# ReLU² attention, Fourier mix and feed-forward on one core: batch 0's rows with a PSUM tile for each half, the first feed-forward groups in two token passes, and the scores of batch 2 held back

## The chip, the cores and the metric

The kernel runs on one core of a Trainium2 chip. The metric is the device time in microseconds (us) of one execution. A core has five engines that run side by side, each through its own list of instructions in a fixed order: PE (matmul), ACT (functions of one operand, with scale and bias), DVE (elementwise work and statistics), POOL (elementwise work and indirect DMA) and SP (which issues DMA). An instruction waits until what it reads is there and what it overwrites is free; all that stands behind it on its engine waits with it. PE writes to PSUM, which is small: here it holds three tiles of two banks, called psS, and two tiles of one bank, called psF.

## The reference

```python
batch, n_heads, seq, head_dim = (8, 12, 448, 64)          # d_model 768, w_ch1 768x3072, w_ch2 3072x768

def _attn_ref(q, k, v):
    scores = scale * np.matmul(q, k.transpose(0, 1, 3, 2))  # scale = 1/sqrt(64)
    attn = np.maximum(scores, 0.0) ** 2 / S
    return np.matmul(attn, v)

def _moe_ref(x, w_ch1, w_ch2):                             # x: the heads side by side, (8, 448, 768)
    mixed = np.real(np.fft.fft(np.fft.fft(x, axis=1), axis=2))
    u = x + mixed
    un = (u - mean(u)) / np.sqrt(var(u) + 1e-06)           # over the last axis
    ch = np.maximum(un @ w_ch1, 0.0) @ w_ch2
    return u + ch
```

## The kernel before

For each batch the kernel computes scores (L537), ReLU on ACT (L558), the square on DVE (L564) and the product with v (L522) for six pairs of heads. `fold` (L445 to L456) turns the result into x with channels on partitions, xT, and into sums and differences of mirrored tokens. The Fourier transform of real data is symmetric, so both transforms are matmuls with half-size cosine and sine tables: over the channels (L961, result copied to `pc`, L977), then over the tokens (L805 in `mix_rows`). A tile of rows stands for a range of tokens from the first half of the sequence ("top", HS = 224 tokens) and its mirror image ("bottom"). For batches 1 to 7 `mix_rows` makes tm, tp, u = x + mixed, its statistics (L837), the scale and the shift (rstd, nmr L846), and the normalized `un` (ACT for batch 1, POOL for later ones, L854). u and un are stored to DRAM (utop and ntop by SP; ubot and nbot by an indirect DMA of POOL that puts the mirrored rows in order, L879).

The feed-forward part, `ffn`, takes tokens in groups: group 0 is the first 384 tokens of batch 0, group 1 the last 64 of batch 0 and all 448 of batch 1, and so on in pairs of 384 and 512. Its input is unT, with channels on partitions. For batches 2 to 7 it comes by a transposing DMA (L902, from ntop and nbot) issued by SP; SP also issues the transposes of x (xn<-xT, L477) and of q and k (qkT<-qkr, L398), the reloads of u into `o` (L1034) and the stores of the output (L1061). For batches 0 and 1 PE transposes un by a matmul with an identity `ident` or a mirrored identity `rev` (L708, L775), and DVE or ACT copy the result to unT (L723, L780). FFN1 (L1073) has 24 blocks of 6 matmuls; each block fills one psF bank with 384 or 512 columns, and a ReLU (L1044 on DVE, L1046 on ACT) writes hT. FFN2 (L1091) accumulates 24 matmuls of 384 columns into a psF bank; DVE adds u (L1054).

Batch 0 has a tail of its own, `first_tail`, because nothing else can run on PE until its first rows are ready. There are four tiles of rows, t = 0 to 3: top tokens 0 to 127 and their mirror, then 112 more of each. `rows` makes both halves (of 384 channels) of a tile into one psS tile (t = 0 to 2) or the two psF banks (t = 3): per half 4 matmuls of 384 columns (L605) and 3 of 128 (L609) that add x. `stats` (L629), `aggregate` (L635), `root` (ACT, L641), `scale` (L649, L650), `copy` (u to SBUF, L658), `norm` (POOL L682, ACT L684, DVE L687), `turn` (transposes, L708) and `unload` (copy to unT, L723) follow, in an order written out by hand. `turn` also issues matmuls on a constant tile `warm` whose result is used by nobody:

```python
for i in range(k):                     # k = 5 in turn 1, 3 in turn 2: 256 columns each (L706)
    nc.tensor.matmul(bank[0][:, 0:256], lhsT=warm[:, 0:128], rhs=warm[:, 0:256], ...)
for i in range(16 if t == 1 else 0):   # 128 columns each (L713)
    nc.tensor.matmul(bank[0][:, 384:512], lhsT=warm[:, 0:128], rhs=warm[:, 0:128], ...)
```

The order on each engine elsewhere is decided when the program is built, by a planner, `Streams`. Each part of the kernel is a generator that asks by `need(engine, duration, dependencies, buffers, condition)` for its next step; the planner takes the step that can start earliest by its own reckoning, a step whose condition is false only if nothing else is left, and on a tie the smaller rank. The durations are estimates in the code, for a matmul of n columns `mm(n)` = n/2400 + 0.006. `progress` counts the feed-forward work planned so far, and attention of a batch may run ahead of it by LEAD. Attention of batch 1 is held while the tail is being written out (`tail[0]` is 1).

Of the kernel before, what the change touches and what calls it, by code (L numbers as in the profile page):

```python
# [117 lines left out]
def mm(n):  # L118
    return n / 2400 + 0.006
# [18 lines left out]
def kernel(  # L138
# [54 lines left out]
    back = [const.tile([128, 1], mybir.dt.int32, name=f"back{i}") for i in range(2)]  # L193
    warm = const.tile([128, 512], BF16, name="warm")
# [27 lines left out]
    def mirrors():  # L222
        nc.gpsimd.memset(rev, 0.0)
        nc.gpsimd.affine_select(out=rev, in_=rev, compare_op=ALU.not_equal, fill=1.0,
                                base=-127, pattern=[[1, 128]], channel_multiplier=1)
        nc.gpsimd.iota(back[0], pattern=[[0, 1]], base=HS, channel_multiplier=-1)

        v = const.tile([128, 2], FP32, name="backv")
# [253 lines left out]
    def attention(b):  # L482
# [5 lines left out]
        while pa < NB:  # L488
# [23 lines left out]
            e = yield need("PE", dur + SWITCH, deps, bufs, lambda: progress[0] >= lead and (b != 1 or tail[0] == 2 or tail[0] == 0 and p < 0))  # L512
# [68 lines left out]
    def first_tail(pcs):  # L581


        pus, helds, done, sts = [None] * 4, [None] * 4, [[None, None] for _ in range(4)], [None] * 4
        mvs, stds, rss, nms, uts, pts = ([None] * 4 for _ in range(6))
        t_st, t_mv, t_std, t_rn = ([0.0] * 4 for _ in range(4))
        t_un, t_u = [[0.0, 0.0] for _ in range(4)], [[0.0, 0.0] for _ in range(4)]

        def rows(t):
            ch, i = divmod(t, 2)  # L590
            s0, s1 = SC[ch]
            n = s1 - s0
            d = 4 * mm(D // 2) + 3 * 0.06
            e = yield need("PE", 2 * d, [pcs[0][1], pcs[1][1]] + x_ready[0], [BF, BF] if t == 3 else [BS])
            if t == 3:
                pu = helds[t] = [BF.take() for _ in range(2)]
            else:
                helds[t] = [BS.take()]
                pu = [helds[t][0][:, 0], helds[t][0][:, 1]]
            for hf in range(2):  # L600

                for w in range(2):
                    for a, (n0, n1) in enumerate(TC):
                        mat = seq[:n1 - n0, w, a, s0:s1] if w == 0 or i ^ hf else nseq[:n1 - n0, a, s0:s1]
                        nc.tensor.matmul(pu[hf][:n, 0:D // 2], lhsT=mat,  # L605
                                         rhs=pcs[a][0][:n1 - n0, w, hf:hf + D // 2],
                                         start=(w == 0 and a == 0), stop=False)
                for a in range(3):
                    nc.tensor.matmul(pu[hf][:n, a * 128:(a + 1) * 128],  # L609
                                     lhsT=xTc[5 - a if hf else a][:, i * XH + s0:i * XH + s1],  # L610
                                     rhs=rev if hf else ident, start=False, stop=(a == 2))
                done[t][hf] = e - (1 - hf) * d + LATENCY["PE"]
            pus[t] = [p[:n] for p in pu]
            if t == 3:
# [5 lines left out]
        def half(t, hf):  # L620

            return pus[t][hf][:, D // 2 - 1::-1] if hf else pus[t][hf][:, 0:D // 2]

        def stats(t, hf):
            n = SC[t // 2][1] - SC[t // 2][0]
            t_st[t] = yield need("DVE", dve(D // 2), [done[t][hf]])
            if hf == 0:
                sts[t] = work.tile([128, 2, 6], FP32, name="stats", tag="stats", bufs=2)
            nc.vector.bn_stats(sts[t][:n, hf, :], pus[t][hf][:, 0:D // 2])  # L629

        def aggregate(t):
            n = SC[t // 2][1] - SC[t // 2][0]
            t_mv[t] = yield need("DVE", 0.2)
            mvs[t] = work.tile([128, 2, 2], FP32, name="mv", tag="mv", bufs=4)[:n]
            nc.vector.bn_aggr(mvs[t][:, 0, :], sts[t][:n])  # L635

        def root(t):
            n = SC[t // 2][1] - SC[t // 2][0]
            t_std[t] = yield need("ACT", 0.25, [t_mv[t] + LATENCY["DVE"]])
            stds[t] = work.tile([128, 2], FP32, name="std", tag="std", bufs=4)[:n]  # L640
            nc.scalar.activation(stds[t][:, 0:1], mvs[t][:, 0, 1:2], AF.Sqrt, bias=eps_t[:n])  # L641

        def scale(t):
            n = SC[t // 2][1] - SC[t // 2][0]
            e = yield need("DVE", 0.3, [t_std[t] + LATENCY["ACT"]])
            t_rn[t] = e + LATENCY["DVE"]
            rss[t] = work.tile([128, 2], FP32, name="rstd", tag="rstd", bufs=4)[:n, 0:1]
            nms[t] = work.tile([128, 2], FP32, name="nmr", tag="nmr", bufs=4)[:n, 0:1]
# [3 lines left out]
        def copy(t, hf, en):  # L652
            ch, i = divmod(t, 2)
            n = SC[ch][1] - SC[ch][0]
            e = yield need(en, (act if en == "ACT" else dve)(D // 2), [done[t][hf]], [BU[i]] if hf == 0 else [])
            if hf == 0:
                uts[t] = work.tile([128, D], FP32, name="u", tag=f"u{i}" if i else "u", bufs=2)
            (nc.scalar.copy if en == "ACT" else nc.vector.tensor_copy)(  # L658
                uts[t][:n, hf * (D // 2):(hf + 1) * (D // 2)], half(t, hf))
            t_u[t][hf] = e  # L660
            if t == 3:
                BF.give(helds[t][hf], e)
            if hf == 1:
                if t != 3:
                    BS.give(helds[t][0], max(t_u[t]))
                e = max(t_u[t])
                first_us[ch][i] = uts[t], e + LATENCY["ACT"], e
                u_done[ch][i].t = e + LATENCY["ACT"]

        def norm(t, hf, en):  # L670
            ch, i = divmod(t, 2)
            n = SC[ch][1] - SC[ch][0]
            deps = [t_rn[t]]
            if en == "POOL":
                deps.append(u_done[ch][i])
            d = {"ACT": act(D // 2), "DVE": dve(D // 2), "POOL": 2.0}[en]
            e = yield need(en, d, deps, [BUN[ch]] if i == 0 and hf == 0 else [])
            if uns[0][t] is None:
                uns[0][t] = work.tile([128, D], BF16, name="un", tag=f"un{t}", bufs=1)
            un = uns[0][t][:n]  # L680
            if en == "POOL":
                nc.gpsimd.tensor_scalar(un, uts[t][:n], rss[t], nms[t], op0=ALU.mult, op1=ALU.add)  # L682
            elif en == "ACT":
                nc.scalar.activation(un[:, hf * (D // 2):(hf + 1) * (D // 2)], half(t, hf), AF.Identity,  # L684
                                     bias=nms[t], scale=rss[t])
            else:
                nc.vector.tensor_scalar(un[:, hf * (D // 2):(hf + 1) * (D // 2)], half(t, hf), rss[t], nms[t],  # L687
                                        op0=ALU.mult, op1=ALU.add)
            t_un[t][hf] = e + LATENCY[en]
            if min(t_un[t]) or en == "POOL":  # L690
                half_un[ch][i].t = max(t_un[t])

        def turned_cols(t):

            return ((128, ident, 0, 128), (128, rev[:, 0:63], HS + 97, 63),
                    (96, ident[:96, :96], 128, 96), (97, rev[:97, 31:128], HS, 97))[t]

        def turn(t, k):
            n, idn, c0, w = turned_cols(t)
            un = uns[0][t]  # L700
            e = yield need("PE", 6 * 0.06 + 0.11 * k, [max(t_un[t])], [BS])
            pts[t] = [BS.take()]
            bank = [pts[t][0][:, 0], pts[t][0][:, 1]]
            for i in range(k):

                nc.tensor.matmul(bank[0][:, 0:256], lhsT=warm[:, 0:128], rhs=warm[:, 0:256], start=True, stop=True)  # L706
            for m in range(MC):
                nc.tensor.matmul(bank[m // 3][:, m % 3 * 128:m % 3 * 128 + w], lhsT=un[:n, m * 128:(m + 1) * 128],  # L708
                                 rhs=idn, start=True, stop=True)
            done[t] = [e + LATENCY["PE"]] * 2  # L710
            for i in range(16 if t == 1 else 0):

                nc.tensor.matmul(bank[0][:, 384:512], lhsT=warm[:, 0:128], rhs=warm[:, 0:128], start=True, stop=True)  # L713
            if t == 1:
                yield need("PE", 16 * 0.055)

        def unload(t, en):
            n, idn, c0, w = turned_cols(t)
            g = groups[0][2]
            src = pts[t][0][:, :, 0:384].rearrange("p h (m w) -> p h m w", w=128)[:, :, :, 0:w]  # L720
            dst = g[:, :, c0:c0 + w].rearrange("p (h m) w -> p h m w", h=2)
            last = yield need(en, (act if en == "ACT" else dve)(6 * w), [done[t][0]])
# [440 lines left out]
```

## Time and profile before

| | before |
|---|---|
| time, median of 3 runs | 610.66 us (610.34 to 611.09) |
| span of the profiled execution | 607.4 us |
| instructions in the profile | 10224 |
| granted PE clock, in every stretch read | 1.000 |
| rows of batch 0 begin on PE | 41.06 us |
| FFN1 of group 0 begins | 53.74 us |
| FFN1 of group 1 begins | 126.67 us |
| FFN1 of group 2 begins | 210.68 us |

The span is that of one profiled execution, from its first to its last instruction; the page gives no other time for it. The median of the runs is 3.26 us longer than the span. All starts below are counted from the start of the span. An engine's share of busy time is an average over the whole span; what a wait costs is read in its place on the timeline.

### The profile page before, as it was taken

How to read it: one execution, taken by the hardware profiler on the slowest of the kernel's cores; microseconds unless marked ns; L12 is line 12 of the kernel's file. 1: busy time of each engine (PE TensorE's matmuls, PEld its weight loads, DVE VectorE, ACT ScalarE, POOL GpSimd, SP SyncE). 2: the span in 40 equal slices, each digit the busy share in tenths (PEclk: the TensorE clock that was granted, in tenths of full speed). 3: DMA queues.
4: the chain of work that ended last, by engine and by line, in shares of the span. 5: the costliest groups of instructions: out<-in, count | busy, mean ns of one | idle time of the engine just before them, and what ended most of it. 6: DMA issues, size and time to landing. Idle time of an engine off the chain costs nothing.

```text
span 607.4 us, 10224 instructions
## 1 busy us (share of the span) xinstructions
PE 595.4 (98%) x4035; PEld 329.5 (54%) x4054; DVE 339.4 (56%) x766; ACT 293.3 (48%) x445; POOL 155.2 (26%) x200
## 2 busy tenths in 40 slices
PE   8999999989999999999999999999999999999997
PEld 7566556534555565555445565555445566654464
DVE  6977785876596568455834369645843447110011
ACT  5967661677544357436653167435761345014300
POOL 8433203311163137111710117210620006100000
PEclk9999999999999999999999999999999999999999
DMA  9999997888659967977593796985451215420022
GB/s 127 207 209 228 216 194 132 186 128 120 111 148 212 157 121 215 141 135 120 172 154 96 127 127 173 160 164 97 145 136 60 87 51 165 121 91 20 1 79 79
DMA packets 125216, 82.22 MB, mean 135 GB/s; under 512 B 76272, under 2 KB 113168, under 8 KB 125168
## 3 DMA queue, kind: packets, MB, share of 16 engines
q0 software_dynamic: 40320, 34.07, 34.4%
q1 hardware_dynamic: 84848, 47.50, 33.6%
q8 instruction: 32, 0.52, 0.4%
q14 instruction: 16, 0.13, 0.1%
HBM read 62.91 MB, written 26.69 MB: 148 GB/s over the span
## 4 chain that ended last, share of the span: by engine, by line
PE 83%; DVE 11%; ACT 4%; issue 1%; DVEq 0%; ACTq 0%
PE psF L1091 33%; PE psF L1073 32%; PE psF L522 6%; PE psS L537 6%; DVE sq L564 2%; PE psS L961 2%; ACT sq L558 2%; DVE stats L837 2%; PE psS L1113 1%; PE psS L805 1%; DVE u L826 1%; DVE u L825 1%; PE psS L605 1%; PE psF L421 1%; DVE tm L816 1%
## 5 line engine op out<-in xcount | busy, mean ns | idle before, releaser
L1073 PE MATMUL psF<-unT,w 128*128 128x384 bf16 (+1 forms) x1134 | 227.2, 352 | 1.4 <-issue 0.2
L558 ACT ACTIVATE sq<-psS 112x896 bf16<-112x896 f32 x192 | 164.8, 916 | 130.5 <-PE psS L537 130.4
L1091 PE MATMUL psF<-w,hT 128*128 128x384 bf16 (+2 forms) x1343 | 225.0, 326 | 0.8 <-DVE xT L448 0.7
L1091 PEld LDWEIGHTS <-hT 128*128 128x128 bf16 x1344 | 129.2, 98 | 93.4 <-issue 8.8
L1073 PEld LDWEIGHTS <-w 128*128 128x128 bf16 x1152 | 109.6, 98 | 109.3 <-issue 12.3
L1046 ACT ACTIVATE hT<-psF 128x512 bf16<-128x512 f32 (+1 forms) x180 | 98.6, 548 | 110.2 <-PE psF L1073 109.6
L564 DVE TENSOR_TENSOR sq<-sq 112x896 bf16<-112x896 bf16 x192 | 117.8, 635 | 44.6 <-ACT sq L558 43.3
L1054 DVE TENSOR_TENSOR o<-psF,o 128x384 f32<-128x384 f32 (+2 forms) x56 | 31.0, 553 | 106.2 <-PE psF L1091 105.9
L300 POOL DMA_DIRECT2D vn<-in_v_dram x24 | 17.3, 719 | 177.4 <-PE psF L522 156.9
L445 DVE TENSOR_SCALAR xT<-psF 128x224 bf16<-128x224 f32 x48 | 18.7, 389 | 71.7 <-PE psF L522 71.7
L537 PE MATMUL psS<-qkT 64*112 64x448 bf16 x384 | 52.3, 366 | 2.0 <-DVE unT L780 0.8
L522 PE MATMUL psF<-sq,vn 112*64 112x448 bf16 x384 | 45.9, 359 | 1.7 <-DVE sq L564 1.2
L825 POOL TENSOR_TENSOR u<-tp,xn 128x385 f32<-128x385 f32 (+1 forms) x14 | 15.5, 1108 | 117.0 <-DVE tp L816 94.7
L537 PEld LDWEIGHTS <-qkT 64*112 64x112 bf16 x384 | 20.8, 125 | 27.6 <-issue 21.6
L522 PEld LDWEIGHTS <-vn 112*64 112x64 bf16 x384 | 17.9, 109 | 24.2 <-issue 16.0
L854 POOL TENSOR_SCALAR un<-u,rstd,nmr 128x768 bf16<-128x768 f32 (+1 forms) x24 | 26.9, 1124 | 6.4 <-DVE nmr L846 6.0
L837 DVE BATCH_NORM_STATS2 stats<-u 128x6 f32<-128x384 f32 (+1 forms) x56 | 28.2, 539 | 0.0
L879 POOL DMA_INDIRECT ubot<-u,back x16 | 17.1, 1072 | 23.7 <-DVE hT L1044 19.3
L300 POOL DMA_DIRECT2D qn<-in_q_dram x21 | 15.3, 726 | 19.7 <-DVE qkr L389 10.8
L1113 PE MATMUL psS<-warm 128*128 128x126 bf16 (+1 forms) x204 | 17.9, 242 | 1.3 <-DVE warm L215 1.3
L448 DVE TENSOR_SCALAR xT<-psF 128x224 bf16<-128x224 f32 x48 | 18.4, 384 | 0.0
L456 DVE TENSOR_TENSOR fold<-xT 128x225 bf16<-128x225 bf16 x48 | 15.9, 331 | 2.1
(117 smaller groups left out, 369.1 us busy)
## 6 DMA issues: line engine op xcount, KB each, us to landing
out_dram<-o SPq DMA_DIRECT2D x27, 384.0 KB, 2.7
vn<-in_v_dram POOLq DMA_DIRECT2D x24, 224.0 KB, 5.0
qn<-in_q_dram POOLq DMA_DIRECT2D x21, 224.0 KB, 6.3
kn<-in_k_dram POOLq DMA_DIRECT2D x21, 224.0 KB, 7.2
w<-in_moe_w_ch_dram POOLq DMA_DIRECT2D x12, 384.0 KB, 14.1
w<-in_moe_w_ch_dram POOLq DMA_DIRECT2D x4, 1152.0 KB, 22.7
utop<-u SPq DMA_DIRECT2D x8, 384.0 KB, 2.6
o<-utop SPq DMA_DIRECT2D x8, 384.0 KB, 4.5
```

Of the source, the lines that this page charges most:

```text
L300: nc.gpsimd.dma_start(out=t, in_=src[b, hs].rearrange("h (p j) d -> p h (j d)", j=4))
L522: nc.tensor.matmul(av[h * Dh:(h + 1) * Dh, 0:S], lhsT=vn[:, c, h0 + h, :], rhs=sq[:, h, :], start=(c == 0), stop=(c == 3))
L537: nc.tensor.matmul(sc[:R, h, 0:S].rearrange("k (c q) -> k c q", c=4), lhsT=kT[ps, m % 2, c, :], rhs=qT[ps, m % 2], start=True, stop=True)
L558: nc.scalar.activation(r, sc[:R, :, 0:S], AF.Relu)
L564: nc.vector.tensor_tensor(r, r, r, op=ALU.mult)
L837: nc.vector.bn_stats(stats[:n, hf, :], u[:n, hf * (D // 2):(hf + 1) * (D // 2)])
L854: nc.gpsimd.tensor_scalar(un[:n], u[:n], rstd[:n, i:i + 1], nmr[:n, i:i + 1], op0=ALU.mult, op1=ALU.add)
L1046: nc.scalar.activation(h[:, 0:N], ph[:, 0:N], AF.Relu)
L1054: nc.vector.tensor_tensor(o[:, hs], pc[:, 0:w], o[:, hs], op=ALU.add)
L1073: nc.tensor.matmul(ph[:, 0:N], lhsT=w1_sb[m][hf][:, jj * 128:(jj + 1) * 128], rhs=unT[:, m, 0:N], start=(m == 0), stop=(m == MC - 1))
L1091: nc.tensor.matmul(pc[:, 0:w], lhsT=hT[j][:, c * 128:(c + 1) * 128], rhs=w2_sb[j // 6][:, j % 6, hs], start=(j == 0), stop=(j == JC - 1))
L1113: nc.tensor.matmul(first_pps[0][:, t, c0:512], lhsT=warm[:, 0:128], rhs=warm[:, c0:512], start=not begun, stop=False)
```

## The change

- In batch 0's tail `rows`, `turn` and `unload` work on halves of a tile. Tile 0 takes the two psF banks, tile 1 two psS tiles (one for each half), tiles 2 and 3 one psS tile each for both halves. The tiles have 128, 128, 96 and 96 tokens, without the overlap that the old ones had. The transposed halves go back to the bank that held the rows.
- The matmuls on `warm` in `turn` are gone.
- The norms of tiles 0 and 1 are ACT's (first half) and DVE's (second half), those of tiles 2 and 3 POOL's. The order is written by hand for tiles 0 and 1, with the first halves of tile 2's work; tiles 2 and 3 are two streams each, `copies` and `later`, for the planner. u is stored tile by tile (`store`) with two new index tiles, `first_back`.
- Groups 0 and 1 hold the tokens in another order, in segments; `reload` and the output store of these groups are cut into pieces.
- FFN1 of group 0 runs as 24 blocks of 128 columns, four blocks to a psF bank and to a ReLU, once tile 0 is ready, and then as 24 blocks of 256 columns, two to a bank. FFN1 of group 1 runs in two passes of 256 columns, the first once the first three transposes are there. hT is six tiles of four blocks instead of 24 tiles.
- Attention of batch 2 is held until the rows of batch 1 are normalized, that of batch 1 until the tail's written order has been planned.
- The planner's `mm(n)` is n/2400 + 0.002.

```diff
-    return n / 2400 + 0.006
+    return n / 2400 + 0.002
...
-  lambda: progress[0] >= lead and (b != 1 or tail[0] == 2 or tail[0] == 0 and p < 0))
+  lambda: progress[0] >= lead and (b != 1 or tail[0] == 2) and (b != 2 or un_ready[1][1].t is not None))
...
+        widths = (128, 128, R - 16, R - 16)
...
+        def rows(t, hf):
+            pool = BF if t == 0 else BS
+            e = yield need("PE", 4 * mm(D // 2) + 3 * 0.06, [pcs[0][1], pcs[1][1]] + x_ready[0],
+                           [pool] if t < 2 or hf == 0 else [])
+            if t < 2 or hf == 0:
+                held[t].append(pool.take())
+            pu = held[t][-1][:n] if t == 0 else held[t][-1][:n, hf if t > 1 else 0]
...
+        def norm(t, hf):
+            if hf is None:
+                e = yield need("POOL", 1.1, [t_rn[t], copied[t]])
+                nc.gpsimd.tensor_scalar(uns[t], uts[t][:widths[t]], rss[t], nms[t], op0=ALU.mult, op1=ALU.add)
+                return
+            en = ("ACT", "DVE")[hf]
...
+        def turn(t, hf):
+            e = yield need("PE", 3 * 0.06, [t_un[t][hf]])
+            for m in range(3 * hf, 3 * hf + 3):
+                nc.tensor.matmul(banks[t][hf][:, m % 3 * 128:m % 3 * 128 + n], lhsT=uns[t][:, m * 128:(m + 1) * 128],
+                                 rhs=rev[:n, 128 - n:] if t % 2 else ident[:n, :n], start=True, stop=True)
...
+        def later(t):
+            for hf in range(2):
+                yield from stats(t, hf)
+            yield from aggregate(t)
+            yield from root(t)
+            yield from scale(t)
+            yield from norm(t, None)
+            for hf in range(2):
+                yield from turn(t, hf)
+            for hf in range(2):
+                e = yield from unload(t, hf)
...
+        yield from run(((rows, 0, 0), (stats, 0, 0), (rows, 0, 1), (copy, 0, 0), (stats, 0, 1), (aggregate, 0),
+                        (copy, 0, 1), (root, 0), (rows, 1, 0), (stats, 1, 0), (scale, 0), (norm, 0, 0), (norm, 0, 1),
+                        (rows, 1, 1), (stats, 1, 1), (aggregate, 1), (rows, 2, 0), (turn, 0, 0), (turn, 0, 1),
+                        (copy, 1, 0), (root, 1), (copy, 1, 1), (scale, 1), (unload, 0, 0), (unload, 0, 1), (rows, 2, 1),
+                        (norm, 1, 0), (norm, 1, 1), (turn, 1, 0), (turn, 1, 1), (unload, 1, 0), (unload, 1, 1)))
         tail[0] = 2
+        for t in (2, 3):
+            if t == 3:
+                for hf in range(2):
+                    yield from rows(t, hf)
+            sch.add(copies(t), (0.05 * t, 0.05 * t))
+            sch.add(later(t), (0.05 * t, 0.05 * t))
...
-            for t0, n in ((0, 384), (384, 512)):
-                groups.append((t0, n, work.tile([128, MC, 512], BF16, name="unT", tag="unT", bufs=2)))
+            for segs, n in (([(0, 128), (HS + 96, 128), (128, 128)], 384), ([(256, 64), (S, 128), (S + HS + 97, 127), (S + 128, 96), (S + HS, 97)], 512)):
+                groups.append((segs, n, work.tile([128, MC, 512], BF16, name="unT", tag="unT", bufs=2)))
...
-        group_ready[0].t = max(c.t for c in first_un)
+        group_ready[0].t = first_un[0].t
...
+        def first(k, c0, w, ready=()):
+            for j0 in range(0, JC, k):
+                for i in range(k):
+                    e = yield need("PE", 6 * mm(w), [w1_ready[hf]] + list(ready),
+                                   ([] if i else [BF]) + ([BH[q]] if hT[q] is None else []))
+                    for m in range(MC):
+                        nc.tensor.matmul(ph[:, i * w:(i + 1) * w], lhsT=w1_sb[m][hf][:, jj * 128:(jj + 1) * 128],
+                                         rhs=unT[:, m, c0:c0 + w], start=(m == 0), stop=(m == MC - 1))
+                sch.add(relu(ph, e, j0, k, c0, w, c0 + w == N), (0, 0))
...
+        if b == 0:
+            yield from first(4, 0, 128, first_un[:1])
+            e = yield from first(2, 128, 256, first_un)
+        elif b == 1:
+            yield from first(2, 0, 256)
+            e = yield from first(2, 256, 256, second_un)
+        else:
+            e = yield from first(1, 0, N)
```

More of the change, by code (lines that the diff above doesn't have):

```diff
@@ L581, in first_tail @@
     def first_tail(pcs):
[L584 to L589, printed above, removed]
-            ch, i = divmod(t, 2)
[L591 to L614, printed above, removed]
@@ L670, in norm @@
[L670 to L691, printed above, removed]
@@ L693, in turned_cols @@
[L693 to L722, printed above, removed]
-            (nc.scalar.copy if en == "ACT" else nc.vector.tensor_copy)(dst, src)
-            BS.give(pts[t][0], last)
-            first_un[t].t = last + LATENCY["ACT"]
+            cp(uts[t][:widths[t], hf * (D // 2):(hf + 1) * (D // 2)], half(t, hf))
@@ L727, in first_tail, with run @@
+        def run(steps):
+            for step, t, *hf in steps:
+                yield from step(t, *hf)
         tail[0] = 1
@@ L906, in turn_un @@
         if b == 1:
+            yield need("SP", 0.0, second_un[:3])
+            group_ready[1].t = max(c.t for c in second_un[:3])
             yield need("SP", 0.0, second_un)
```

256 lines of the change are left out of this document (143 added, 113 removed).

## The prediction

> **What bounds the kernel now.** I read the page first, then the waits of PE, then PE's timeline around batch 0's tail and batch 1's rows, then ACT and DVE beside it, and last SP's queue for group 2.
>
> Parts 1 and 4 of the page (busy time; chain by engine and line):
>
> ```profile
> PE 595.4 (98%) x4035; PEld 329.5 (54%) x4054; DVE 339.4 (56%) x766; ACT 293.3 (48%) x445; POOL 155.2 (26%) x200
> PE 83%; DVE 11%; ACT 4%; issue 1%; DVEq 0%; ACTq 0%
> ```
>
> PE is busy 595.4 of 607.4 us, at a granted clock of 1.000 in every stretch that I read. So the change can pay in two ways only: fewer columns through PE, or fewer PE waits. The waits of PE (total, times, longest):
>
> ```profile
> PE psF L522 <- DVE sq L564: 1.2, 2, 1.0
> PE psS L708 <- ACT un L684: 0.9, 1, 0.9
> PE psS L537 <- DVE unT L780: 0.8, 1, 0.8
> PE psF L522 <- ACT hT L1046: 0.5, 1, 0.5
> PE psS L537 <- DVE unT L723: 0.4, 1, 0.4
> ```
>
> L708, L723 and hT are batch 0's tail (48 to 66 us); L780 and most of sq are batch 1's rows (119.9 to 125.4). A record runs some 0.16 us past the start of its successor (L609 at 42.03 lasts 0.33, the next starts at 42.20), so a listed wait costs its length and 0.16 more. PE's timeline, first in batch 0's tail and then at batch 1's rows (start, length, instructions, [idle before]):
>
> ```profile
> 48.00 0.50 PE L708 MATMUL psS<-ident,un 128*128 128x128 bf16 x6
> 48.33 0.71 PE L706 MATMUL psS<-warm 128*128 128x256 bf16 x5
> 48.88 0.34 PE L708 MATMUL psS<-rev,un 128*128 128x63 bf16 x6
> 49.05 1.06 PE L713 MATMUL psS<-warm 128*128 128x128 bf16 x16
> 49.94 0.49 PE L706 MATMUL psS<-warm 128*128 128x256 bf16 x3
> 50.27 0.42 PE L708 MATMUL psS<-ident,un 96*128 96x96 bf16 x6
> 51.60 0.44 PE L708 MATMUL psS<-rev,un 97*128 97x97 bf16 x6 [0.91 <-ACT un L684]
> ...
> 122.58 0.40 PE L537 MATMUL psS<-qkT 64*112 64x448 bf16 x2 [0.83 <-DVE unT L780]
> 124.89 0.38 PE L522 MATMUL psF<-sq,vn 112*64 112x448 bf16 x2 [1.04 <-DVE sq L564]
> ```
>
> **The change, part by part.** Differences are made against the profiled execution's span, 607.4 us; the median of the runs, 610.66, lies 3.26 above it and that is added at the end. Where an instruction falls in the changed kernel I take from its built order on each engine.
>
> *Dummies out.* 5+3 of L706 and 16 of L713 take 48.33 to 48.88, 49.05 to 49.94 and 49.94 to 50.27: 0.55+0.89+0.33 = 1.77 us of PE. They are ahead of the 0.91 wait, so leaving them out alone would only lengthen that wait; it pays because FFN1's first pass (24x6 matmuls of 128 columns) needs only tile 0 and can fill the time.
>
> *Smaller pieces of FFN1.* Group 0 moves 144x128+144x256 columns for 144x384, group 1 288x256 for 144x512: the same columns. A matmul of 384 takes 0.1655 us (48 of L1091 from 200.20 to 208.11, a block of scores and values apart), six of 128 with six different weights 0.33 (L708 at 48.00), 0.055 each: proportional, so nothing. Against this stands the weight load, 98 ns a piece: if that bound a 128-column matmul, 144x(0.098-0.055) = +6.2 us. L708 with its changing weights speaks against it, over six only. The Trainium skill, "TensorE: Matmul & The Clock Gate", section "Wait — 56ns, not 53.3ns?", has a fixed 2.5 ns per matmul beside the columns: with 260 more matmuls in the whole kernel an estimate of +0.65 us. The rows here show no such part.
>
> *The tail's waits.* In the old order, the waits after the rows are 0.91, 0.35 and 0.51, with 0.16 each 2.25 us. In the new one the rows again start at 41.06 (nothing ahead moves). Walking the new order with durations of rows (a row half 0.83; ACT copy 0.48; statistics 0.57, two in 1.03; root 0.30; reciprocal and nmr 0.30; norm 0.68 a half; POOL norm 0.98; unload of a half 0.48 on ACT, 0.54 on DVE): turn 0 waits 0.12, and FFN1's first pieces 0.26 and 0.33 on unloads. Tiles 2 and 3 still share one PSUM tile for both halves, and there ACT and DVE take turns. The old row for that, from the timeline of ACT: a copy of one half held behind the statistics of the other:
>
> ```profile
> 44.37 0.48 ACT L658 COPY u<-psS 128x384 f32<-128x384 f32 x1 [1.30 <-DVE stats L629]
> ```
>
> So copy, statistics, copy, statistics run one after another (4 steps, 2.1 us, a tile), and DVE, now the only engine for the qkT copy of batch 1 (0.61), comes to it at 53.2. PE's next transposes need that copy's bank: PE is through with its FFN1 pieces at 51.6 and waits until 53.85, 2.28 us. Behind it: 0.20, 0.17 and 0.33 in the scores' and values' buffers. Sum 3.69, that is +1.44 on the old 2.25. With the dummies that makes -0.33. Counted another way, by the work PE has behind it at 71.5, the new kernel has 5376 more FFN1 columns (2.31 us), but two pairs of scores (0.70) and one block of values (0.88) fewer: -0.73. The second count holds every wait, named or not, so I take -0.75 and keep 0 and -2.2 (the 2.28 wait as short as the old 0.91) as ends. The Trainium skill, "PSUM — Partial Sum Buffer", section "PSUM bank collisions raise a hardware error", asks only that two engines keep out of one bank; by it copy and statistics of tiles 2 and 3 could run side by side, since the halves lie in two banks, and the tail would come out at its lower end (rival 1). The 1.30 above is an order by PSUM tile, stricter than that.
>
> *Batch 1's rows, scores of batch 2 held.* The old waits are 0.83, 1.04, 0.15 and 0.16, with 0.16 each 2.8 us, all from DVE and ACT doing unloads, squares and statistics at once. The hold takes the squares out: FFN2 of group 0 then ends 16.2 us after batch 1's mix starts, and FFN1 of group 1, whose first 256 tokens need only the first three turns, can start at 18.5, when DVE has unloaded tile 0's turn behind the second pair's statistics, while PE is free at 16.9 after a turn of 0.7: a wait of 1.6, some 1.85 with small ones (2.6 if two more statistics go ahead). Counted by columns, as at 71.5, the old stretch (118 to 126.7) loses 3.0: gain 1.15 (0.2 to 2.8).
>
> *What the hold costs.* Batch 2's attention is moved behind batch 1's rows, and its mix is now followed by group 2's FFN1 after 35.85 us of PE work; before it had 52.8 (mix at 157.9, FFN1 at 210.68). Group 2's rows go through SP's queue. Old rows of its timeline, and under them the landings of all unT transfers (L902):
>
> ```profile
> 187.22 0.38 SPq L876 DMA_DIRECT2D ntop<-un  x1
> 190.03 1.21 SPq L477 DMA_TRANSPOSE xn<-xT  x1
> 193.40 1.26 SPq L902 DMA_TRANSPOSE unT<-ntop  x1
> 196.79 1.23 SPq L902 DMA_TRANSPOSE unT<-nbot  x1
> ...
> DMA to landing us min/median/max: 2.5/4.3/8.9
> ```
>
> In the new order unT<-ntop stands behind an xn<-xT of batch 3, which waits for a block of values that ends 28.9 us after the mix. Then 0.9 for xT, 1.2 and 1.3 for two transposes: nbot is issued at 32.3 and lands at 36.6 by the median, 38.8 with the 6.5 of the one at 216.8. PE arrives at 35.85 and 0.8 for waits in the mix (DVE's o add behind squares), 36.65. The wait is 0 to 3.4 us; the median says 0, a crowded queue more, and I take 1.0. Old waits in that stretch (158 to 211) are 0.76 of idle, 1.2 with 0.16 for three; new 0.8+1.0: +0.6.
>
> *The rest*: the smaller hT tiles, the pieces of out and o (more DMAs on SP, hidden since an o add is due 10 us later), ACT's and POOL's share of norms: off PE's path, nothing; from 211 us on the order is the old one.
>
> Sum: -0.75-1.15+0.6 = -1.3, a span of 606.1 and a time of 609.4.
>
> **Rivals.**
> 1. *Group 2 is in time and the waits of rows go as intended.* For it: batch 3's chain, from its mix (218.3) to nbot issued (244.3) and landed 5.3 later, takes 31.3, under 36.65. Then -2.2 in the tail to -0.75, -1.15 to -2.0, and -0.4 in group 2: -2.3 to -4.6, 606.1 to 608.4. Against it: the place in SP's queue.
> 2. *Slower: group 2 comes late.* With its issue held as the one of 244.30, which took 3.26 us where others take 1.25, and a landing of 6.5, nbot is there at 40.8, PE waits 4.15 and the time is 612.5; with a landing of 8.9 and no hold 41.2, 613.0. It decides from a landing 40.1 us after the mix (a wait of 3.5) on, which gives 611.9. For it: those rows, and SP's queue, where more pieces of out and o now stand. Against: the median.
> 3. *The halves are not freed at all*: the shared PSUM tile of tiles 2 and 3 delays POOL's norms too, and FFN1's second pass waits for all four tiles. Each us it takes is lost; walked, the second pass starts at 58.6, when PE has other work until then. Another 1.5 us: 610.9.
> 4. *Weight loads bound the 128-column pass*: +6.2, 615.6.
> 5. *The clock.* Dummies kept PE from idling; here 1.28 us of idle in 41 to 54 us left the clock at 1.000, and 2.28 at a piece is longer than any wait shown. If it fell to half for as long as a wait of some 3 us, that is +1.5 or more: 610.9. The Trainium skill, "TensorE: Matmul & The Clock Gate", section "Why this matters for your kernels", asks for no idle gap over about 3 us; 2.28 is inside it.
>
> **How the numbers follow.** Forecast, with its ends 608.4 to 610.8: 0.40, half of it below 609.44, where faster by over 0.2% begins (0.2%, 1.2 us, is about what this kernel's measurement can tell from no change). Rival 1: 0.23, faster. Rival 2: 0.23, slower. Rivals 3 and 5: 0.08, at 610.9 within 0.2%, but with a second late wait above 611.9: half and half. Rival 4: 0.06, slower. Faster 0.20+0.23 = 0.43; slower 0.23+0.04+0.06 = 0.33; same 0.24. The range leaves out rival 4 and the outermost ends: 605.9 to 613.2.
>
> **What would show it.** Right: no dummies of L706 and L713; PE waits near 52 us on DVE's qkT copy, about 2.3; no wait over 1 near 123; one wait of up to 3 us ahead of group 2's FFN1, released by unT<-nbot; 128-column matmuls 0.055 apart. Wrong: 0.098 apart; any wait over 2 us elsewhere; a granted clock below 1; a group 2 that starts without a wait while the time doesn't fall.

## The result, and the profile after

The changed kernel takes 631.42 us (630.79 to 632.18, 5 runs) against 610.45 us for the kernel before (609.58 to 611.09, 5 runs): a ratio of 1.0347, 95% interval 1.0331 to 1.0363. It is 21 us slower, far outside the range that was given. All times here and below are medians and ranges of undisturbed runs; one run of experiment 4 (e4_even_nohold, 627.66 us) was disturbed and is left out. The profiled execution has a span of 629.0 us, 21.6 more than before.

The chain of the changed kernel's page (in this kernel FFN1 is L1083, FFN2 L1111, scores L540, values L525):

```profile
PE 82%; DMA 6%; DVE 6%; issue 2%; POOL 2%; ACT 2%; SPq 1%; DVEq 0%; ACTq 0%; POOLq 0%
```

DMA, which had no share before, now has 6%. The waits of PE (total, times, longest):

```profile
PE psF L1111 <- DVE o L1054: 8.6, 1, 8.6
PE psS L540 <- DMA qkT<-qkr: 3.9, 1, 3.9
PE psF L1083 <- DVE sq L567: 2.3, 1, 2.3
PE psF L424 <- DVE qkT L429: 1.9, 1, 1.9
PE psF L1083 <- ACT std L829: 1.2, 1, 1.2
```

The last two are the tail and batch 1's rows, near the forecast (2.28 and 1.6). The first three, 14.8 us, lie in one stretch, 201 to 228 us. PE's timeline there, and in the tail:

```profile
51.05 0.51 PE L1083 MATMUL psF<-unT,w 128*128 128x128 bf16 x6
53.45 0.39 PE L424 MATMUL psF<-ident,qn 112*64 112x112 bf16 x8 [1.89 <-DVE qkT L429]
54.48 3.58 PE L1083 MATMUL psF<-unT,w 128*128 128x128 bf16 x36
59.96 3.86 PE L1083 MATMUL psF<-unT,w 128*128 128x128 bf16 x66
...
210.41 5.05 PE L1111 MATMUL psF<-w,hT 128*128 128x384 bf16 x18 [8.59 <-DVE o L1054]
219.70 0.99 PE L540 MATMUL psS<-qkT 64*112 64x448 bf16 x4 [3.91 <-DMA qkT<-qkr]
```

What PE waited for at 210.41, from the timelines of DVE and of SP (SP's column of lengths is the time that an issue took):

```profile
209.80 0.56 DVE L1054 TENSOR_TENSOR o<-psF,o 128x384 f32<-128x384 f32 x1 [10.71 <-DMA o<-ubot]
```

```profile
189.02 0.23 SPq L1032 DMA_DIRECT2D o<-ubot  x1
189.37 6.80 SPq L864 DMA_DIRECT2D ntop<-un  x1
196.27 9.75 SPq L401 DMA_TRANSPOSE qkT<-qkr  x1
```

A reload of u, issued at 189.02, was not there until 209.8, 20.7 us later; the two issues behind it on SP took 6.80 and 9.75 us where others take 0.4 and 1.3. It is the last reload of group 1, in two pieces: 31 rows of utop (issued at 188.34) and 97 rows of ubot (291 KB). The new order of group 1's tokens cuts its last two tiles at 63 and 65, and at 31 and 97 rows. The trace's DMA packets show how the last tile came in: its 128 rows of 3 KB start one after another, the first at 190.06 and the last at 209.20, some 0.15 us apart. Stretches of the changed kernel (busy time of PE, PEld, DVE, ACT and POOL with counts, then granted clock, DMA share, GB/s):

```profile
54.00:57.40 3.40, 3.40 (x36) 3.38 (x35) 1.24 (x5) 1.21 (x2) 2.86 (x3) 0.50 1.26 205
200.00:210.00 10.00, 1.82 (x16) 0.77 (x15) 0.20 (x1) 2.53 (x3) 0.12 (x1) 0.71 0.07 22
204.20:214.43 10.23, 4.02 (x13) 1.92 (x13) 0.56 (x1) 0.00 (x0) 0.00 (x0) 0.50 0.62 75
217.84:224.67 6.83, 4.97 (x20) 1.82 (x22) 4.89 (x12) 1.73 (x2) 0.01 (x1) 0.50 0.60 127
228.09:231.50 3.41, 3.41 (x14) 1.41 (x14) 0.42 (x1) 0.89 (x2) 0.00 (x0) 0.50 1.40 180
```

From 200 to 210 us the DMA share is 0.07, about one engine of 16. And the granted clock, 1.000 in the profiled execution of the kernel before, is 0.50 in four stretches. In them PE is busy for 3.40, 4.02, 4.97 and 3.41 us, half of which, 7.9 us, the full clock would not have needed.

So of 21.6 us the three waits take 14.8 (15.3 with 0.16 each), the half clock 1.7 in the tail and 6.2 around group 2. That is 23.2; by subtraction the rest of the change is worth -1.6, beside the -1.9 that the prediction had for the tail and batch 1's rows. No run shows this rest by itself, and experiment 6 does not bear it out.

### The profile page after: what moved, and what is told of

The parts are those of the page before. It is cut to its first block, busy times and chain, and to the rows that moved or that the text cites. A ratio compares the mean times of both kernels' runs of the same rounds, so it can differ in the third digit from the quotient of the medians.

```text
span 629.0 us, 10756 instructions
## 1 busy us (share of the span) xinstructions
PE 602.7 (96%) x4314; PEld 352.8 (56%) x4314; DVE 338.3 (54%) x766; ACT 295.5 (47%) x446; POOL 154.1 (24%) x201
## 4 chain that ended last, share of the span: by engine, by line
PE 82%; DMA 6%; DVE 6%; issue 2%; POOL 2%; ACT 2%; SPq 1%; DVEq 0%; ACTq 0%; POOLq 0%
PE psF L1111 35%; PE psF L1083 32%; PE psF L525 6%; PE psS L540 6%; PE psS L952 2%; DMA w<-in_moe_w_ch_dram 2%; DMA qkT<-qkr 2%; DMA qn<-in_q_dram 1%; PE psS L793 1%; DVE stats L825 1%; DVE sq L567 1%; DMA vn<-in_v_dram 1%; DVE u L814 1%; SPq L401 1%; POOL qk L303 1%
## 5 line engine op out<-in xcount | busy, mean ns | idle before, releaser
L1083 PE MATMUL psF<-unT,w 128*128 128x256 bf16 (+3 forms) x1440 | 232.7, 318 | 5.0 <-DVE sq L567 2.3
L1111 PE MATMUL psF<-w,hT 128*128 128x384 bf16 (+2 forms) x1344 | 228.2, 329 | 8.6 <-DVE o L1054 8.6
L1111 PEld LDWEIGHTS <-hT 128*128 128x128 bf16 x1344 | 130.1, 98 | 103.6 <-issue 21.4
L1083 PEld LDWEIGHTS <-w 128*128 128x128 bf16 x1440 | 133.9, 99 | 96.6 <-issue 17.5
L540 PE MATMUL psS<-qkT 64*112 64x448 bf16 x384 | 52.7, 369 | 4.6 <-DMA qkT<-qkr 3.9
L525 PE MATMUL psF<-sq,vn 112*64 112x448 bf16 x384 | 46.5, 365 | 0.1
L813 POOL TENSOR_TENSOR u<-tp,xn 128x385 f32<-128x385 f32 (+1 forms) x14 | 15.3, 1094 | 109.9 <-DVE tp L804 98.2
L540 PEld LDWEIGHTS <-qkT 64*112 64x112 bf16 x384 | 20.5, 126 | 29.7 <-issue 20.0
L525 PEld LDWEIGHTS <-vn 112*64 112x64 bf16 x384 | 18.1, 110 | 22.3 <-issue 14.7
L1133 PEld LDWEIGHTS <-warm 128*128 128x128 bf16 x206 | 13.6, 108 | 6.3 <-issue 4.6
L867 POOL DMA_INDIRECT ubot<-u,back x14 | 14.8, 1056 | 5.2 <-DMA ubot<-u,back 2.2
```

Of the source, the lines that this page charges most:

```text
L525: nc.tensor.matmul(av[h * Dh:(h + 1) * Dh, 0:S], lhsT=vn[:, c, h0 + h, :], rhs=sq[:, h, :], start=(c == 0), stop=(c == 3))
L540: nc.tensor.matmul(sc[:R, h, 0:S].rearrange("k (c q) -> k c q", c=4), lhsT=kT[ps, m % 2, c, :], rhs=qT[ps, m % 2], start=True, stop=True)
L1083: nc.tensor.matmul(ph[:, i * w:(i + 1) * w], lhsT=w1_sb[m][hf][:, jj * 128:(jj + 1) * 128], rhs=unT[:, m, c0:c0 + w], start=(m == 0), stop ...
L1111: nc.tensor.matmul(pc[:, 0:w], lhsT=hT[j // 4][:, j % 4, c * 128:(c + 1) * 128], rhs=w2_sb[j // 6][:, j % 6, hs], start=(j == 0), stop=(j ...
L1133: nc.tensor.matmul(first_pps[0][:, t, c0:512], lhsT=warm[:, 0:128], rhs=warm[:, c0:512], start=not begun, stop=False)
```

## The experiments

**1. The uneven rows, in the changed kernel** (e1_even).

```diff
 def pieces(c, bounds=False):
-                out.append((r, t, w))
-                r += w
+                for n in ((w // 16 * 16, w % 16) if w % 16 else (w,)):
+                    out.append((r, t, n))
+                    r, t = r + n, t + n
```

> The changed kernel, but every piece of an o reload or output store whose row count is no multiple of 16 is cut in two, the largest multiple of 16 and the rest (97 = 96+1, 65 = 64+1, 63 = 48+15, 31 = 16+15). Theory A (a DMA of 97 rows is carried row by row by one of the 16 DMA engines, and what shares that engine queues behind it): the o<-ubot reload lands in under 8 us instead of 20.7, the PE waits of 8.6 us (DVE o) and 3.9 us (qkT<-qkr) and the half clock after 204 us are gone; the stretch from 201 to 232 us lost 21.5 us of PE time in the changed kernel, of which the forecast's 1 to 2 may stay, so 631.4-19.5 to 631.4-21.5 = 610 to 612 us. Theory B (the transposes and the indirect stores of batch 2's rows, moved next to each other by the held scores, block each other on SP's queue): the long issues of ntop<-un (6.8) and qkT<-qkr (9.75) stay, time over 625 us.

Measured: 619.98 us (615.68 to 621.36), ratio 1.0156 (1.0128 to 1.0184), span 618.4. The reload no longer stands in the way, and the waits of 8.6 and 3.9 us are gone; but 610 to 612 was missed, since another wait stands there now. PE's timeline, SP's and DVE's:

```profile
216.38 4.00 PE L1084 MATMUL psF<-unT,w 128*128 128x384 bf16 x12 [7.13 <-DMA unT<-nbot]
```

```profile
205.50 1.19 SPq L480 DMA_TRANSPOSE xn<-xT  x1
207.44 1.34 SPq L890 DMA_TRANSPOSE unT<-ntop  x1
208.87 1.25 SPq L890 DMA_TRANSPOSE unT<-nbot  x1
```

```profile
204.45 0.43 DVE L392 COPY qkr<-kn 112x1024 bf16<-112x1024 bf16 x1 [3.16 <-DMA qkT<-qkr]
```

It is the wait for group 2's rows, which in the changed kernel lay behind the waits of the long reload: nbot's transpose is issued 36.7 us after batch 2's mix (172.21), behind an xn<-xT whose xT stands on DVE behind a copy that waits 3.16 us for a buffer, and lands 7.5 us later. The clock is 0.50 from 211.2, inside this wait, to 221.4, with PE busy 5.0 us in it: 2.5 us more.

**2. The uneven rows alone, in the kernel before** (e2_before_97), with a control whose cut lies one row further (e2b_before_96).

```diff
 def reload(c):                      # the kernel before, one tile of group 1
                 w = min(HS - r, end - t)
+                if b == 1 and c == 3 and w == 128:
+                    w = 31          # in the control: 32
```

> The kernel before, with one edit: the last o reload of group 1 (128 rows of ubot in one DMA, issued at 196.14) is cut into 31 and 97 rows. Theory A: the 97 rows take 15 to 21 us, landing at 212 to 217 where the o adds of that tile begin at some 205, so PE stalls for want of a psF bank by 3 to 8 us, the clock may fall with it: 614 to 622 us. Theory B: the same bytes in two DMAs instead of one, landing in 4 to 7 us: 610 to 611 us.

> Control for e2_before_97: the same reload of the kernel before cut at the same place, into 32 and 96 rows, so that only the divisibility differs. Theory A (the uneven row count puts a DMA on one engine): nothing is late, 609 to 611 us, against the 624.6 us of 31 and 97 rows. Rival (two DMAs instead of one, or the place of the cut, make it late): 615 us or more.

Measured: 31+97 rows take 624.63 us (623.69 to 625.75), ratio 1.0243 (1.0223 to 1.0263); 32+96 rows take 610.50 us (609.14 to 611.98), ratio 1.0003 (0.9988 to 1.0018). SP's timeline with 97 rows, and with 96:

```profile
197.46 0.87 SPq L1036 DMA_DIRECT2D o<-ubot  x2
198.42 17.65 SPq L902 DMA_TRANSPOSE unT<-nbot  x1
```

```profile
197.84 0.99 SPq L1036 DMA_DIRECT2D o<-ubot  x2
198.92 1.23 SPq L902 DMA_TRANSPOSE unT<-nbot  x1
```

With 97 rows, what DVE and PE waited for, and the stretch at half clock in the columns used above:

```profile
220.34 0.56 DVE L1056 TENSOR_TENSOR o<-psF,o 128x384 f32<-128x384 f32 x1 [15.61 <-DMA o<-ubot]
PE psF L522 <- DVE o L1056: 11.8, 1, 11.8
213.50:227.10 13.60, 6.15 (x25) 2.65 (x25) 4.08 (x11) 2.53 (x3) 0.00 (x0) 0.50 0.41 100
```

One row more or less in a cut is worth 14 us: the next issue on SP takes 17.65 us instead of 1.23, the o add waits 15.6 us for the reload, PE waits 11.8 us, and of the 6.15 us that PE is busy in the 13.6 us at half clock another 3.1 are lost. The DMA packets show why: with 31+97 the 128 rows start one after another from 199.67 to 219.76, with 32+96 all of them start between 199.11 and 200.88. Theory A is shown, and its price was underestimated (614 to 622 expected). Both 31 and 97 are uneven here, as in the changed kernel, and all 128 rows pass in one line; no run has 97 uneven rows alone.

**3. The clock.** First the constant-tile matmuls out of the kernel before (both loops to range(0), e7_before_nodummy); then such matmuls put into the changed kernel's gap (e3_even_dummy).

> The kernel before without the 24 matmuls on the constant tile in the tail (1.77 us of PE), nothing else. If they are there to keep the clock: PE idles some 2.7 us in 48.3 to 51.6, the clock is granted at 0.5 for 3.4 us after it, and the time is up by 1 to 1.8 us: 611.5 to 612.5. If they only fill a wait that ACT's norm sets: 1.000 throughout and 610.0 to 610.8 us.

Measured: 610.93 us (610.10 to 612.05), ratio 1.0020 (1.0010 to 1.0031) to a before of 609.3 in that comparison, 1.2 us by the ratio. PE's timeline and, in the columns used above, the stretch after it:

```profile
49.75 0.43 PE L708 MATMUL psS<-ident,un 96*128 96x96 bf16 x6 [1.28 <-POOL un L682]
51.15 0.44 PE L708 MATMUL psS<-rev,un 97*128 97x97 bf16 x6 [0.97 <-ACT un L684]
```

```profile
52.90:56.30 3.40, 3.40 (x26) 1.58 (x28) 2.03 (x4) 1.46 (x3) 0.00 (x0) 0.52 1.19 222
```

Where 1.77 us of constant-tile matmuls stood there is now a wait of 1.28 us, and the wait for ACT's norm stays (0.97 for 0.91). So the last transposes start 3.77 us after the last matmuls of the rows, as in the kernel before: nothing is gained, and the half clock is on top. The time lies between the two ranges; the granted clock speaks for the first, and not in the profile alone: all 11 runs have a mean clock of 0.994 to 0.997, where 11 of 17 runs of the kernel before have 1.000.

```diff
 def turn_on_pe(b, g):               # on top of experiment 1
+            if b == 1 and g == 1 and r == 1:
+                e1 = yield need("PE", 30 * 0.055, [], [BS], lambda: tail[0] == 2)
+                d = BS.take()
+                for _ in range(30):
+                    nc.tensor.matmul(d[:, 0, 0:128], lhsT=warm[:, 0:128], rhs=warm[:, 0:128], start=True, stop=True)
+                BS.give(d, e1)
```

> e1_even with 30 matmuls of 128 columns on the constant tile ahead of the transposes for which PE waited 1.9 us in the tail (53.45 us). Theory (idle PE time in a stretch of some 3.4 us halves the clock for the next 3.4 us): no granted clock of 0.5 in 50 to 60 us, FFN1 matmuls there 0.055 apart instead of 0.10; gain of up to 1.5 us on e1_even, less what the matmuls delay (up to 1.5): e1_even -1.5 to 0. Rival (the clock falls for another reason, such as many small matmuls): half clock in 54 to 58 us stays, and the time is e1_even +0 to +1.5.

Measured: 621.39 us (620.37 to 623.49), ratio 1.0202 (1.0184 to 1.0220). The clock stays 1.000 from 50 to 60 us, as the theory has it (in experiment 1 it is 0.83 there), but the time is 1.4 us above experiment 1, not below:

```profile
52.93 1.83 PE L420 MATMUL psS<-warm 128*128 128x128 bf16 x30 [1.44 <-ACT sq L567]
50.00:60.00 10.00, 8.56 (x154) 7.39 (x153) 5.93 (x17) 6.31 (x13) 3.08 (x3) 1.00 1.18 222
```

The matmuls wait 1.44 us for a psS tile themselves, push batch 1's scores back, and new waits for squares appear at 206 us. The 1.4 us is not clear of noise (experiment 1 ran from 615.68 to 621.36). That idle time brings on the half clock is shown by the first of the two kernels; the second agrees but proves little, since e6_even_unt_act (experiment 5) has the same wait of 1.9 us in the tail as experiment 1 and its profile shows 1.000 there. The remedy is none.

**4. The hold, out of the kernel of experiment 1** (e4_even_nohold) **and into the kernel before** (e9_before_hold).

```diff
-  ... and (b != 2 or un_ready[1][1].t is not None))     # e4_even_nohold, against e1_even
+  ... and (b != 2 or un_ready[1][1].t is not None))     # e9_before_hold, against the kernel before
```

> e1_even without the condition that holds batch 2's scores. In e1_even PE has 37 us of work between batch 2's mix (172.21) and FFN1 of group 2, and the rows are there 44 us after the mix (unT<-nbot landed at 216.3), so it waits 7.1 us and then runs at half clock for 10 us. By the built order this kernel has 41.8 us of work there. Theory H (the hold makes the wait): the wait shrinks by some 5 us to about 2, the half clock after it is gone (2.6), batch 1's rows wait 1.4 us more than with the hold: 612 to 615 us. Rival (the transfers are late whatever the order, so that the wait moves along): 618 us or more.

Measured: 616.61 us (614.45 to 619.19), ratio 1.0111 (1.0081 to 1.0141), span 613.2. Nothing waits ahead of group 2, and the clock stays full there; batch 1's rows wait 2.5 us for ACT instead, more than expected. By the profile theory H holds: the wait is gone. The time is 1.6 us above its range, and the gain of 3.4 us on experiment 1 is not clear of noise, since the two intervals overlap.

> The kernel before with one part of the change alone: the scores of batch 2 held until batch 1's rows are normalized. By its built order PE has 43.4 us of work between batch 2's mix and FFN1 of group 2 (53.0 without the hold). Theory H: the waits at batch 1's rows (2.8 us) shrink by 1 to 2 us, and with rows ready 44 us after the mix a wait of 0 to 3 us appears ahead of group 2: 608.5 to 612 us. Rival (the hold by itself costs what was seen in e1_even): a wait of 5 us or more and half clock, 615 us or more.

Measured: 606.87 us (606.53 to 610.63), ratio 0.9958 (0.9940 to 0.9975). The waits of L780 and of sq at batch 1's rows are gone from the list of PE's waits, whose first lines are now

```profile
PE psS L1113 <- DVE warm L215: 1.3, 1, 1.3
PE psS L708 <- ACT unT L723: 1.0, 1, 1.0
PE psF L1091 <- DVE xT L448: 0.6, 1, 0.6
```

Group 2's FFN1 starts 43.6 us after the mix without a wait. This part alone beats both kernels, and the time is 1.6 us under the range of theory H: the waits at batch 1's rows went almost wholly, and no new one came ahead of group 2. Then the hold only until the first half (e15_before_hold0):

```diff
-  ... and (b != 2 or un_ready[1][1].t is not None))     # against e9_before_hold
+  ... and (b != 2 or un_ready[1][0].t is not None))
```

> e9_before_hold with the scores of batch 2 released already when the first half of batch 1's rows is normalized. By its order PE has 49.0 us of work between batch 2's mix and FFN1 of group 2 (43.4 in e9_before_hold, where no wait was seen), so nothing more is to be gained there; at batch 1's rows squares come back between the unloads of the second half. Theory (what the hold gives is the stretch 118 to 127 us): 607 to 609 us, between e9_before_hold (606.87) and before. Rival (the first half's statistics and unloads are all that matters): equal to e9_before_hold or up to 1 us faster.

Measured: 607.50 us (606.02 to 610.49), ratio 0.9956 (0.9940 to 0.9972): as good as the full hold. Squares between the second half's unloads cost nothing that shows.

**5. What makes group 2 late.** First the transposes moved to ACT's queue (e6_even_unt_act), then the planner's number (e11_even_mm6), then the loads beside the transfer (e17_even_late_loads); each on e1_even.

```diff
-            e = yield need("SP", 1.5, deps, bufs)
+            e = yield need("ACT" if b == 2 else "SP", 1.5, deps, bufs)
-            nc.sync.dma_start_transpose(out=g[...], in_=src[...])
+            (nc.scalar if b == 2 else nc.sync).dma_start_transpose(out=g[...], in_=src[...])
```

> e1_even with the two transposes unT<-ntop and unT<-nbot of group 2 issued by ACT instead of SP; nothing stands ahead of them there but squares. In e1_even nbot landed in DRAM at 204.7 and its transpose was issued at 208.87, behind an xn<-xT that waited until 205.50 for DVE. Theory Q (the place in SP's queue sets the wait): issued near 205 and landed near 212, the wait of 7.1 falls to 2 to 4 us: e1_even -4 to -7. Rival L (the transfers themselves are slow in this stretch): lands at 215 or later as before, and ACT loses what it waits: e1_even -1 to +2.

Measured: 624.23 us (622.63 to 625.21), ratio 1.0236 (1.0209 to 1.0262). Neither theory: ACT issued ntop's transpose at 205.65 and nbot's only at 216.44, and the squares stood behind them, so that PE waited 11.5 us for squares. It says nothing about SP's queue.

```diff
-    return n / 2400 + 0.002
+    return n / 2400 + 0.006
```

> e1_even with one number changed: the planner's mm back at n/2400+0.006, the hold kept as in the change. By the built order PE then has 44.5 us of work between batch 2's mix and group 2's FFN1 instead of 36.7. In every kernel so far nbot's transpose was issued 36 to 39 us after the mix and landed 4 to 7.5 us later, at 41 to 44. Theory (the work between mix and FFN1 decides against a chain of 41 to 44 us): wait of 0 to 1 us in place of 7.1, no half clock after it, 618.4 - 7.1 - 2.6 = 608.7 in the span: 609 to 612 us. Rival (the chain grows with the hold whatever the planner's number): a wait over 3 us, 614 us or more.

Measured: 615.61 us (613.91 to 616.17), ratio 1.0087 (1.0068 to 1.0107). PE arrives later by the 8 us expected, and the wait falls from 7.1 to 3.0, not to 0 to 1: nbot's transpose is issued 40.0 us after the mix, and PE starts 8.2 us after that (PE's list of waits names no releaser here; the landing is taken as the cause). So part of the rival is true: the chain is longer too.

```diff
+            if x == 2 and i == 13:          # the v load issued at 208.84
+                for _ in range(4):
+                    nc.gpsimd.memset(t, 0.0)
             nc.gpsimd.dma_start(out=t, in_=src[b, hs].rearrange(...))
```

> e1_even with four POOL memsets of the v buffer (which the load then overwrites) ahead of the loads vn, qn and kn that POOL issued at 208.84, 209.53 and 210.23, in the same microsecond as the transpose unT<-nbot (208.87). They begin when the buffer is free, as the load did, and hold the three loads back by some 3 to 5 us. In the runs so far nbot's transpose landed within 4.2 us where these loads came 1.9 us after it (e4_even_nohold), and took 7.5 and 8.2 us where they came with it or 0.9 us ahead (e1_even, e11_even_mm6). Theory (the loads' packets on the DMA engines slow the transpose): landing 4 to 5.5 us after issue, the wait ahead of group 2 falls from 7.1 to 4 to 5, less half clock after it: e1_even -2 to -4. Rival (the transpose is slow for another reason): landing 7 us or more, e1_even -0.5 to +1.

Measured: 615.31 us (613.04 to 616.17), ratio 1.0076 (1.0048 to 1.0105). The three loads come at 211.97 to 213.35, and PE's timeline has

```profile
212.33 4.00 PE L1087 MATMUL psF<-unT,w 128*128 128x384 bf16 x12 [4.00 <-DMA unT<-nbot]
```

The transpose, issued at 208.43, landed by 212.33: 3.9 us instead of 7.5. The wait ahead of group 2 falls by 3.1 of 7.1 us, so the loads of batch 4, issued within 1.4 us of the transpose, were nearly half of it. The time fell by 4.7 us, more than the 2 to 4 expected.

**6. All causes mended at once** (e14_all): even pieces, hold until the first half, mm at 0.006, and the rows of tile 3 behind the first transposes of batch 1.

```diff
             if t == 3:
+                yield need("SP", 0.0, [go])     # go: set when PE's transposes of batch 1, group 1, r = 0 are planned
                 for hf in range(2):
                     yield from rows(t, hf)
```

> The changed kernel with four edits: even pieces as in e1_even; scores of batch 2 released when the first half of batch 1's rows is normalized; the planner's mm back at 0.006 (48.8 us of work between batch 2's mix and group 2's FFN1 by its order); the rows of tile 3 placed behind the first transposes of batch 1, so that PE works where it waited 1.9 us. If the three causes found so far (uneven DMA, rows of group 2 late, idle time that halves the clock) are all of the loss: no PE wait over 1.5 us after 45 us, clock 1.000 to the end, and 608 to 610 us, the forecast's sum without its group 2 term. If something else is left: above 612 us.

Measured: 610.96 us (608.97 to 613.99), ratio 1.0014 (0.9996 to 1.0032). The 20 us are back, so the three causes are nearly all of the loss. Against the expectation PE still waits for xT:

```profile
215.32 2.12 PE L1087 MATMUL psF<-unT,w 128*128 128x384 bf16 x12 [2.08 <-DVE xT L453]
```

The clock falls in eight of twelve runs, and the kernel is 3.5 us behind e15_before_hold0, which has the same hold and planner number. So what is left of the change (the new tail, the passes of FFN1, the new pieces) costs time here, taken together. The clock is not the reason: the two profiles, 610.0 and 606.4 us, each have one piece at half clock in the tail and the same mean clock, 0.997. Nor is the work: PE is busy 596.7 and 596.8 us. The 3.6 us are idle time, of which the lists of waits name 2.1 us for xT against 1.2 and 1.6 for ReLUs of hT against 0.5. Which part of the change brings them was not taken apart.

## Why the prediction was wrong, step by step

- *"The rest: ... the pieces of out and o (more DMAs on SP, hidden since an o add is due 10 us later)"* is the step that failed worst. It counted DMAs and never asked how long a DMA of 97 rows takes; all DMAs of u and o that SP issued before had 32, 64, 96 or 128 rows, so no row of the trace priced it. The 10 us of slack were right: the reload was issued at 189.02, and DVE began to wait for it 10 us later. The landing was not: it came after 20.7 us, which cost 8.6 us of PE's time at once, and the same cut costs 14 us when it is put into the kernel before alone. The Trainium skill, "DMA: Bandwidth & Descriptors", section "Why a DMA increments its semaphore by 16 and not by 1", says it: the number of engines is the largest up to 16 that divides the row count on both sides, and for 127 partitions one engine is left. The trace agrees (31+97 rows start one after another, at a DMA share of 0.07). That page was not weighed, and it was the rule that spoke against this change.
- *Group 2's wait, "nbot is issued at 32.3 and lands at 36.6 by the median"*: the mechanism was right, the size was not. Where SP issues it and no long reload stands ahead, the issue came 36 to 40 us after the mix in the profiles, and the landing 4 to 8 us later. In experiment 1, where PE arrived 37.0 us after the mix (36.65 forecast), the wait put at 1.0 was 7.1, above the 4.15 to 4.55 of rival 2. The prediction's own fence had the better row: the old kernel issued that transpose at 196.79, 38.9 us after its mix. It took a walk of SP's queue for the price and left out that DVE's queue, too, stands behind a transfer (3.16 us for a qkr buffer), and that the loads of batch 4 meet the transpose.
- *The clock, rival 5, 0.08 with rival 3*: right in kind, and too unlikely in the forecast. It looked for a wait of 3 us; the half clock came after a wait of 1.89 us in the changed kernel's profile, and after two of 1.28 and 0.97 in experiment 3. The Trainium skill's bound of about 3 us ("TensorE: Matmul & The Clock Gate", "Why this matters for your kernels"), which the prediction leaned on, is too wide for this case; the measurement decides. The price named, 1.5 us or more, was 1.7. It was also not carried over to the long waits elsewhere, where it cost 6.2 us more.
- *The tail's waits*: 0.12, 0.26, 0.33 and 2.28 were forecast; at 47.29 a wait of 0.27 and at 53.45 one of 1.89 (2.06 by starts) are there, on DVE's qkT copy as said. That the tail is worth -0.75 is not borne out: the half clock there cost 1.7, and without the three causes (experiment 6) the kernel is behind, not ahead. No run has the new tail alone.
- *Batch 1's rows*: a wait of 1.6 was forecast, 1.23 (1.39 by starts) came. The gain was put at 1.15; the hold alone makes the kernel before 0.42% faster, some 2.6 us, so it was worth more.
- *Weight loads*: rightly given little. 66 matmuls of 128 columns take 3.79 us (59.96 to 63.75), 0.0574 each, not 0.098. But "the rows here show no such part" was wrong. From start to start the median matmul of the changed kernel's trace takes 56 ns for 128 columns in that stretch and 163 ns for 384, so three small ones take 5 ns more than a large one. This is the fixed part of some 2.5 ns a matmul that the Trainium skill ("TensorE: Matmul & The Clock Gate", "Wait — 56ns, not 53.3ns?") has; the sum took nothing for it, where the prediction's own estimate was 0.65 us.
- *Rival 2, "slower: group 2 comes late"* had the place and the sign. Its price, up to 613.0, stopped at one late landing. Without the uneven reload, with the wait of 7.1 us and the half clock around it, the time is 620 us (experiment 1); with the reload it is 631.

## What to carry to other kernels

When a change cuts tensors into other pieces, price each DMA by its row count first: here 31 and 97 rows, which no number from 2 to 16 divides, passed row by row, and all that was issued behind them on the queue waited as well; cutting them into 16+15 and 96+1 undid it. Moving work behind a wait shortens the slack of whatever came later, so take the length of that later chain from its own old row, not from a walk of one queue. And a PE wait of a microsecond or two can cost up to half of the next 3.4 us again, through the clock.

## What the runs showed of the hardware

- A DMA that passes row by row blocks the queue that issued it: the next issue on SP took 17.65 us (experiment 2). Loads from POOL's queue were late too: in the changed kernel the loads of q and k issued in that stretch landed 16.9 and 19.2 us later.
- The half clock comes in pieces of 3.4 us, and one piece costs some 1 to 2 us, the wait ahead of it included: of ten runs of the kernel before in the last comparison, six at a mean granted clock of 1.000 took 608.85 to 609.34 us, two at 0.997 610.41 and 611.07, two at 0.994 612.10 and 613.21.
- Among waits under 2 us no length decides it in these traces. The old tail's waits (0.91 and 0.35) left the clock at 1.000 in the profile of the kernel before and brought a piece in that of e15_before_hold0. Waits of 0.8 and 1.0 at batch 1's rows brought one in the profile of the control of experiment 2, and none in the kernel before. The new tail's 1.9 brought one in five of six profiles.
- A transpose of group 2's rows landed in 3.9 us when the first of three loads of 224 KB was issued 3.5 us after it, and in 7.5 us with the three issued beside it.
